# Raw keys and values for block maxima and sums: loads set 12 steps ahead of their batch, each sum in the step after its load

## The chip, the core and the metric

The kernel runs on one core of a Trainium2 chip. The core has TensorE (PE) for matrix products, VectorE (DVE), ScalarE (ACT) and GpSimd (POOL) for elementwise work, and SyncE (SP), which here only issues DMA transfers. Each engine works through its own list of instructions in order and waits for others by semaphores. The metric is the device time of one execution in microseconds. A change of less than 0.2% cannot be told from none here.

## The reference

Attention over a window and block summaries, followed by a feed-forward layer with a rational activation:

```python
# q, k, v: batch 4, heads 8, sequence 768, head size 64; block 32, window 16
k_sum = k.reshape(B, H, nb, block, D).max(axis=3)       # 24 block maxima of the keys
v_sum = v.reshape(B, H, nb, block, D).mean(axis=3)      # 24 block means of the values
scores_l = scale * q @ k^T, kept where |i - j| < 16
scores_s = scale * q @ k_sum^T + log(32)
a = softmax over both sets of scores
attn = a @ concat(v, v_sum)                             # 3072 tokens x 512
h = x @ w_in                                            # 512 -> 2048
P = a0 + a1*h + a2*h^2 + a3*h^3
Q = 1 + |b0|*|h| + |b1|*h^2
out = (P / (Q + 1e-6)) @ w_out                          # 2048 -> 512
```

## The kernel before

**Tiles.** The 3072 tokens are six groups of 512. The hidden width of 2048 is 16 slices (fc) of 128. A *step* is one slice of one group: `moe1` makes h (128x512) by twelve products, `gelu` turns it into a high and a low part gh and gl, and three steps later (`LAG`) `moe2` adds their products with the second weight matrix to the four output tiles po. So there are 96 steps and three more, numbered from 0; step 16 g + fc is tile `h{g}_{fc}`. A gelu is six passes of VectorE (L312, L315 to L319), five of ScalarE (L309 to L311, L313, L314) and one of GpSimd (L320, gl). The buffers of h, ta, tq and tu are double.

**Attention.** It runs in 48 half-blocks (jj) of 64 queries, 12 to a batch. The first eight are done ahead of step 0 (the ramp); the others are spread over the steps by `start_of(jj)`: two steps apart from half-block 16 on. In its step, a half-block's scores (sc) are multiplied, VectorE adds the mask and takes minima (L180), ScalarE exponentiates (L184), VectorE takes the reciprocal of the sums (L186, L187), GpSimd scales (L189, ss). In the next step TensorE transposes ss (L207, pt), once ahead of each output tile of `moe2`; the step after, the values are averaged (av).

**Block maxima and sums.** Batch 0 uses keys resident since the ramp. For batch 1, 2 and 3, `key_sum` loads four raw key tiles kr (128x768, 384 KB) and reduces each to 24 maxima (L118). For batches 2 and 3, `value_sum` loads four tiles vr (96x1024, 384 KB) and adds blocks of 32 (L126); batch 1 has its averages from TensorE. Keys of a batch are wanted when its first half-block is scored, at `start_of(12 bi)`: steps 7, 30 and 54; the values two steps later.

**Staging.** kr, vr, the halves of the weight slices 8 to 15 (wr, 512 KB each) and the outputs o of groups 0 to 4 share one pool `stage` of two buffers of 4 KB per partition, taken in turn. A half of a weight slice is rescaled by ScalarE (L281), shifted and joined by VectorE (L284, L285), copied by ScalarE (L288) and its remainder taken by GpSimd (L290).

**Order.** A scheduler places the instructions of each engine by priority and by its own estimate of when data is there. TensorE's list is pinned: `mm` and the transposes are held in the order in which they are written (`tc.keep_in_program_order`, which puts an instruction behind the one last written for its engine). VectorE's list is left to the scheduler. `todo` holds what is done beside the products of a step, entered by `at(step, function, ...)` and executed by `run` in three slots; `PRIO` shifts the priority of a function, and the sums are 15 places lower than they are written:

```python
KOFF = 6
VOFF = 5
PRIO = {"key_sum": -15, "value_sum": -15, "half_a": 40, "att_c": 40}
```

So the four key sums of batch 2 are written in steps 24 to 27 and the value sums in 25 to 28, those of batch 3 in 48 to 51 and 49 to 52, and those of batch 1 in 1 to 4; where they stand is the scheduler's choice.

Of the kernel before, what the change touches and what calls it, by code (L numbers as in the profile page):

```python
# [8 lines left out]
F32 = mybir.dt.float32  # L9
# [9 lines left out]
NB = S // BLK  # L19
# [23 lines left out]
NEARLY = 3  # L43
KOFF = 6
VOFF = 5
VLAG = 5
# [6 lines left out]
SLOT = {"att_c": 0, "half_a": 0, "att_b": 1}  # L53
PRIO = {"key_sum": -15, "value_sum": -15, "half_a": 40, "att_c": 40}
NHALF = NT // HQ
# [3 lines left out]
def tile_kernel(ctx, tc, qw_in, kraw, kwin, vpad, vred, wio, a, b, cmask, cident, cavg, out):  # L59
# [48 lines left out]

    def key_sum(bi, pr):
        if pr == 0:  # L110
            ksum[bi] = sp.tile([P, NPAIR, NB], F32, tag="ks", name=f"ks{bi}", bufs=2)
        if bi == 0:
            nc.sync.dma_start(out=kres[:, pr, :], in_=kraw[bi, pr])
            kr = kres[:, pr, WIN:WIN + S]
        else:
            kr = stage.tile([P, S], F32, tag="st", name=f"kr{bi}_{pr}")
            nc.sync.dma_start(out=kr, in_=kraw[bi, pr, :, WIN:WIN + S])
        nc.vector.tensor_reduce(ksum[bi][:, pr, :], kr.rearrange("p (n k) -> p n k", k=BLK), axis=AX.X, op=ALU.max)  # L118

    def value_sum(bi, c):  # L120
        if c == 0:
            vsum[bi] = sp.tile([NB * 4, NVC, VD], F32, tag="vs", name=f"vs{bi}", bufs=2)
        vs = vsum[bi]
        vr = stage.tile([NB * 4, VD, BLK], F32, tag="st", name=f"vr{bi}_{c}")
        nc.sync.dma_start(out=vr, in_=vred[bi, c])
        nc.vector.tensor_reduce(vs[:, c, :], vr, axis=AX.X, op=ALU.add)  # L126
        if c == NVC - 1:
            nc.vector.tensor_scalar_mul(vs, vs, 1.0 / BLK)
# [222 lines left out]
    for what in FIRST.split():  # L351
        n = int(what[1:] or 0)
        if what[0] == "Q":
            first_q(*((0, 2), (2, HPG))[n])
        elif what[0] == "K":
            key_sum(0, n)
        elif what[0] == "S":
# [37 lines left out]
    def run(step, slot):  # L395
        for f, args in todo.get((step, slot), ()):
            with tc.high_priority(offset=PRIO.get(f.__name__, 0)):
                f(*args)
# [12 lines left out]
    for jj in range(HPG, NHALF):  # L411
        at(start_of(jj) + 2, att_c, jj)
        at(start_of(jj), half_a, jj)
        at(start_of(jj) + 1, att_b, jj)
    for bi in range(1, B):
        for k in range(NPAIR):
            at(max(start_of(bi * NJ) - KOFF + k, 0), key_sum, bi, k)
        for k in range(NVC if bi > 1 else 0):
            at(max(start_of(bi * NJ) - VOFF + k, 0), value_sum, bi, k)
    for fc in range(NEARLY, NFC):  # L420
# [79 lines left out]
```

## Time and profile before

| What | Value |
|---|---|
| Median of 3 runs | 741.35 us (740.69 to 742.2) |
| The profiled execution's own time, its span | 740.98 us, 739.2 us |
| TensorE busy | 685.4 us (93%) |
| VectorE, ScalarE, GpSimd busy | 603.1, 471.1, 314.1 us |
| Mean granted TensorE clock | 0.962 |
| HBM read, written | 53.44 MB, 6.34 MB |

The profile is of one execution. Its page gives busy times, slices of the span, DMA queues, the chain of work that ended last, and the costliest groups of instructions; the trace behind it answers for single lines, tiles and stretches. A row of a timeline reads: start in us, duration, engine, line, operation, output and input tiles, count, and in brackets the engine's idle time before it with what ended it. A row of waits reads: who waited for whom, us in total, times, longest. A row of stretches reads: from:to, length, then busy us and instruction count of PE, PEld, DVE, ACT and POOL, the granted clock (1.00 is full), the DMA engines' busy share and GB/s; a stretch table for one line has that line's engine alone. A row of groups has count, busy us, mean ns of one, and the idle time just before them. A row of DMA issues has count, KB each and the median us from issue to landing.

### The profile page before, as it was taken

The numbers are of one execution on the slowest core, as the hardware profiler recorded it, in microseconds if no ns is written. First come the engines' busy times: TensorE is split into PE (matmuls) and PEld (weight loads), VectorE is DVE, ScalarE is ACT, GpSimd is POOL, SyncE is SP. The second block draws the span as 40 slices with busy tenths as digits, with TensorE's granted clock in tenths as the row PEclk, the third lists the DMA queues.
The fourth block names the chain that finished last, engine by engine and source line by source line (L and its number), as shares of the span: only waits on it lengthen the run. The fifth ranks groups of instructions, "written<-read, shape, count | busy, mean of one in ns | idle before, by whom it ended". The sixth has DMA issues, their size and how long they took to land.

```text
span 739.2 us, 12001 instructions
## 1 busy us (share of the span) xinstructions
PE 685.4 (93%) x4196; PEld 529.8 (72%) x4196; DVE 603.1 (82%) x1189; ACT 471.1 (64%) x1058; POOL 314.1 (42%) x328
## 2 busy tenths in 40 slices
PE   7875698899998999997999996999999999999997
PEld 4544476677776777775777775777777777888886
DVE  4588988997988878977778986877987887988885
ACT  2885667776765665774666774566776666675563
POOL 0676556653532444542343442534445343222231
PEclk9986599999999999999999999999999999999999
DMA  9984353512136101133110125111122110010001
GB/s 290 371 276 145 117 168 104 163 40 57 30 120 185 40 30 45 46 97 83 42 46 30 57 72 150 35 49 38 30 72 72 32 37 1 1 58 1 1 1 58
DMA packets 30681, 60.76 MB, mean 82 GB/s; under 512 B 3748, under 2 KB 15396, under 8 KB 29596
## 3 DMA queue, kind: packets, MB, share of 16 engines
q1 hardware_dynamic: 29916, 59.54, 25.5%
q8 instruction: 33, 0.54, 0.3%
q10 hardware_dynamic: 576, 0.25, 0.1%
q14 instruction: 28, 0.23, 0.1%
q0 software_dynamic: 128, 0.20, 0.1%
HBM read 53.44 MB, written 6.34 MB: 81 GB/s over the span
## 4 chain that ended last, share of the span: by engine, by line
PE 65%; DMA 14%; DVE 7%; POOL 5%; ACT 4%; issue 3%; SPq 0%; POOLq 0%; DVEq 0%; ACTq 0%
PE po L77 30%; PE h L77 28%; DMA wr<-in_wio_dram 5%; PE sc L77 4%; DMA kr<-in_kraw_dram 3%; PE av L77 2%; PE pt L207 2%; POOL ss L189 2%; DMA vr<-in_vred_dram 2%; DMA vr<-in_vpad_dram 1%; POOL w L290 1%; POOL wearly L290 1%; DVE tq L312 1%; DMA out_dram<-o 1%; ACT ss L184 1%
## 5 line engine op out<-in xcount | busy, mean ns | idle before, releaser
L320 POOL TENSOR_TENSOR gl<-tu,ta 128x512 fp32r<-128x512 f32 x96 | 133.7, 1393 | 232.3 <-DVE tu L319 145.6
L189 POOL TENSOR_SCALAR ss<-ss,sm 128x120 f32<-128x120 f32 x192 | 132.3, 705 | 143.2 <-ACT ta L314 93.6
L312 DVE SCALAR_TENSOR_TENSOR tq<-tq,cs,ta 128x512 f32<-128x512 f32 x96 | 109.9, 1145 | 51.8 <-ACT ta L310 51.2
L309 ACT ACTIVATE tq<-h 128x512 f32<-128x512 f32 x96 | 57.2, 596 | 133.0 <-PE h L77 131.4
L77 PE MATMUL po<-wearly,gh 128*128 128x512 f32 x384 | 134.3, 432 | 0.0
L77 PE MATMUL po<-w,gh 128*128 128x512 f32 x384 | 127.6, 413 | 0.0
L313 ACT ACTIVATE ta<-tq,cs 128x512 f32<-128x512 f32 x96 | 69.7, 726 | 73.2 <-DVE tq L312 72.3
L77 PE MATMUL h<-xh,wearly 128*128 128x512 f32 x384 | 102.4, 411 | 3.6 <-DVE tu L316 3.2
L77 PE MATMUL h<-xh,w 128*128 128x512 f32 x384 | 95.5, 391 | 0.0
L317 DVE SCALAR_TENSOR_TENSOR gh<-tu,cs,ta 128x512 fp32r<-128x512 f32 x96 | 73.7, 768 | 22.3 <-ACT ta L314 11.9
L77 PEld LDWEIGHTS h<-xh,wearly 128*128 128x128 f32 x384 | 75.2, 197 | 21.6 <-DVE tu L316 3.4
L207 PE MATMUL pt<-ident,ss 128*120 128x128 f32 x192 | 54.8, 296 | 33.2 <-POOL ss L189 31.8
L77 PEld LDWEIGHTS h<-xh,w 128*128 128x128 f32 x384 | 72.1, 188 | 16.1
L77 PEld LDWEIGHTS po<-wearly,gh 128*128 128x128 f32 x384 | 67.5, 198 | 18.0 <-issue 4.9
L319 DVE SCALAR_TENSOR_TENSOR tu<-tu,cs,tq 128x512 f32<-128x512 f32 x96 | 77.3, 806 | 3.0
L184 ACT ACTIVATE ss<-ss,sm 128x120 f32<-128x120 f32 x192 | 73.0, 383 | 10.0 <-DVE sm L180 10.0
L77 PE MATMUL po<-wearly,gl 128*128 128x512 f32 x192 | 78.0, 406 | 0.0
L77 PEld LDWEIGHTS po<-w,gh 128*128 128x128 f32 x384 | 65.7, 190 | 16.9 <-issue 2.7
L77 PE MATMUL po<-w,gl 128*128 128x512 f32 x192 | 75.5, 393 | 0.0
L311 ACT ACTIVATE tu<-h,cs 128x512 f32<-128x512 f32 x96 | 75.0, 781 | 0.0
L316 DVE SCALAR_TENSOR_TENSOR tu<-tu,cs,h 128x512 f32<-128x512 f32 x96 | 71.6, 746 | 2.8
L318 DVE SCALAR_TENSOR_TENSOR tq<-tq,gh 128x512 f32<-128x512 f32 x96 | 68.7, 716 | 2.9
(63 smaller groups left out, 1046.8 us busy)
## 6 DMA issues: line engine op xcount, KB each, us to landing
vw<-in_vpad_dram SPq DMA_DIRECT2D x44, 192.0 KB, 2.8
wr<-in_wio_dram SPq DMA_DIRECT2D x8, 1024.0 KB, 10.4
wr<-in_wio_dram SPq DMA_DIRECT2D x16, 512.0 KB, 4.0
kw<-in_kwin_dram SPq DMA_DIRECT2D x40, 192.0 KB, 2.6
out_dram<-o SPq DMA_DIRECT2D x24, 256.0 KB, 2.1
qw<-in_qw_dram SPq DMA_DIRECT2D x40, 128.0 KB, 2.7
kr<-in_kraw_dram SPq DMA_DIRECT2D x12, 384.0 KB, 3.5
vr<-in_vred_dram SPq DMA_DIRECT2D x8, 384.0 KB, 3.4
```

Of the source, the lines that this page charges most:

```text
L77: ins = nc.tensor.matmul(*args, **kw)
L184: nc.scalar.activation(ss[:, pr, :], ss[:, pr, :], AF.Exp, scale=-1.0, bias=sm[:, 0, pr:pr + 1], accum_out=sm[:, 1, pr:pr + 1])
L189: nc.gpsimd.tensor_scalar(ss[:, pr, :], ss[:, pr, :], sm[:, 1, pr:pr + 1], 1.0, op0=ALU.mult, op1=ALU.mult)
L207: ins = nc.tensor.transpose(out=pt[:NK, pr * P:(pr + 1) * P], in_=ss[:, pr, :], identity=ident)
L311: nc.scalar.activation(tu, h, AF.Identity, scale=cs[:, 3:4], bias=cs[:, 2:3])
L312: nc.vector.scalar_tensor_tensor(out=tq, in0=tq, scalar=cs[:, 5:6], in1=ta, op0=ALU.mult, op1=ALU.add)
L313: nc.scalar.activation(ta, tq, AF.Ln, bias=cs[:, 7:8])
L316: nc.vector.scalar_tensor_tensor(out=tu, in0=tu, scalar=cs[:, 1:2], in1=h, op0=ALU.add, op1=ALU.mult)
L317: nc.vector.scalar_tensor_tensor(out=gh, in0=tu, scalar=cs[:, 0:1], in1=ta, op0=ALU.add, op1=ALU.mult)
L318: nc.vector.scalar_tensor_tensor(out=tq, in0=tq, scalar=C1 * SH, in1=gh, op0=ALU.add, op1=ALU.mult)
L319: nc.vector.scalar_tensor_tensor(out=tu, in0=tu, scalar=cs[:, 0:1], in1=tq, op0=ALU.add, op1=ALU.subtract)
L320: nc.gpsimd.tensor_tensor(gl, tu, ta, op=ALU.mult)
```

## The change

`key_sum` and `value_sum` are each split into a load and a sum. The loads of batch bi are written from `s = start_of(12 bi) - 12` on, one per step: four of keys, then four of values (steps 18 to 25 for batch 2, 42 to 49 for batch 3; 0 to 3 for batch 1, which has keys alone). Each sum is written in the step after its load. It has no lowered priority any more and is pinned on VectorE behind the instruction written before it. In a step, `run` takes loads last.

```diff
-KOFF = 6
-VOFF = 5
+SOFF = 12
...
-PRIO = {"key_sum": -15, "value_sum": -15, "half_a": 40, "att_c": 40}
+LATE = ("key_load", "value_load")
+PRIO = {"half_a": 40, "att_c": 40}
...
+    sums = {}
+
-    def key_sum(bi, pr):
+    def key_load(bi, pr):
         if pr == 0:
             ksum[bi] = sp.tile([P, NPAIR, NB], F32, tag="ks", name=f"ks{bi}", bufs=2)
         if bi == 0:
...
         else:
             kr = stage.tile([P, S], F32, tag="st", name=f"kr{bi}_{pr}")
             nc.sync.dma_start(out=kr, in_=kraw[bi, pr, :, WIN:WIN + S])
-        nc.vector.tensor_reduce(ksum[bi][:, pr, :], kr.rearrange("p (n k) -> p n k", k=BLK), axis=AX.X, op=ALU.max)
-
-    def value_sum(bi, c):
+        sums["k", bi, pr] = kr
+
+    def key_sum(bi, pr):
+        kr = sums.pop(("k", bi, pr))
+        ins = nc.vector.tensor_reduce(ksum[bi][:, pr, :], kr.rearrange("p (n k) -> p n k", k=BLK), axis=AX.X, op=ALU.max)
+        if bi:
+            tc.keep_in_program_order(ins)
+
+    def value_load(bi, c):
         if c == 0:
             vsum[bi] = sp.tile([NB * 4, NVC, VD], F32, tag="vs", name=f"vs{bi}", bufs=2)
-        vs = vsum[bi]
         vr = stage.tile([NB * 4, VD, BLK], F32, tag="st", name=f"vr{bi}_{c}")
         nc.sync.dma_start(out=vr, in_=vred[bi, c])
-        nc.vector.tensor_reduce(vs[:, c, :], vr, axis=AX.X, op=ALU.add)
+        sums["v", bi, c] = vr
+
+    def value_sum(bi, c):
+        vs, vr = vsum[bi], sums.pop(("v", bi, c))
+        tc.keep_in_program_order(nc.vector.tensor_reduce(vs[:, c, :], vr, axis=AX.X, op=ALU.add))
         if c == NVC - 1:
             nc.vector.tensor_scalar_mul(vs, vs, 1.0 / BLK)
...
+            key_load(0, n)
             key_sum(0, n)
...
-        for f, args in todo.get((step, slot), ()):
+        for f, args in sorted(todo.get((step, slot), ()), key=lambda z: z[0].__name__ in LATE):
...
     for bi in range(1, B):
+        s = max(start_of(bi * NJ) - SOFF, 0)
         for k in range(NPAIR):
-            at(max(start_of(bi * NJ) - KOFF + k, 0), key_sum, bi, k)
+            at(s + k, key_load, bi, k)
+            at(s + k + 1, key_sum, bi, k)
         for k in range(NVC if bi > 1 else 0):
-            at(max(start_of(bi * NJ) - VOFF + k, 0), value_sum, bi, k)
+            at(s + NPAIR + k, value_load, bi, k)
+            at(s + NPAIR + k + 1, value_sum, bi, k)
```

The change shifts the line numbers: L118, L126, L180, L187, L312, L315 and L319 become L124, L137, L191, L198, L323, L326 and L330.

VectorE's list around steps 35 and 36 (tiles tq2_3 and tq2_4), before the change, in the middle of which the first two key sums of batch 3 stand:

```order
L312 SCALAR_TENSOR_TENSOR tq2_3_3183<-tq2_3_3183,cs_95,ta2_3_3182 128x512
L315 TENSOR_TENSOR tu2_3_3184<-tu2_3_3184,h2_3_3169 128x512
L316 SCALAR_TENSOR_TENSOR tu2_3_3184<-tu2_3_3184,cs_95,h2_3_3169 128x512
L118 TENSOR_REDUCE ks3_4087<-kr3_0_4088 128x24
L317 SCALAR_TENSOR_TENSOR gh2_3_3185<-tu2_3_3184,cs_95,ta2_3_3182 128x512
L318 SCALAR_TENSOR_TENSOR tq2_3_3183<-tq2_3_3183,gh2_3_3185 128x512
L319 SCALAR_TENSOR_TENSOR tu2_3_3184<-tu2_3_3184,cs_95,tq2_3_3183 128x512
L118 TENSOR_REDUCE ks3_4087<-kr3_1_4140 128x24
L312 SCALAR_TENSOR_TENSOR tq2_4_3236<-tq2_4_3236,cs_95,ta2_4_3235 128x512
```

With the change the same two sums stand at steps 43 and 44. The first is ahead of the gelu of step 44 (tq2_12):

```order
L328 SCALAR_TENSOR_TENSOR gh2_11_3708<-tu2_11_3707,cs_95,ta2_11_3705 128x512
L329 SCALAR_TENSOR_TENSOR tq2_11_3706<-tq2_11_3706,gh2_11_3708 128x512
L330 SCALAR_TENSOR_TENSOR tu2_11_3707<-tu2_11_3707,cs_95,tq2_11_3706 128x512
L124 TENSOR_REDUCE ks3_3689<-kr3_0_3690 128x24
L323 SCALAR_TENSOR_TENSOR tq2_12_3758<-tq2_12_3758,cs_95,ta2_12_3757 128x512
```

The second is behind the reciprocal of that step's half-block (sm31):

```order
L327 SCALAR_TENSOR_TENSOR tu2_12_3759<-tu2_12_3759,cs_95,h2_12_3744 128x512
L197 TENSOR_SCALAR sm31_3794<-sm31_3794 128x4
L198 RECIPROCAL sm31_3794<-sm31_3794 128x4
L124 TENSOR_REDUCE ks3_3689<-kr3_1_3742 128x24
L328 SCALAR_TENSOR_TENSOR gh2_12_3760<-tu2_12_3759,cs_95,ta2_12_3757 128x512
```

The sums of batches 2 and 3 alternate between these two places; they are written one in each of steps 19 to 26 and 43 to 50.

SyncE's list behind the ramp, before: the second and third raw key tiles of batch 1 are followed by the weight slices 7 and 8.

```order
L117 DMA kr1_1_823<-in_kraw_dram 128x768
L117 DMA kr1_2_900<-in_kraw_dram 128x768
L268 DMA wr7_0_826<-in_wio_dram 128x2048
L150 DMA vnext_107<-vn_595 24x512
L195 DMA vw0_100<-in_vpad_dram 96x512
L268 DMA wr8_0_904<-in_wio_dram 128x1024
L268 DMA wr8_1_906<-in_wio_dram 128x1024
L195 DMA vw1_101<-in_vpad_dram 96x512
L117 DMA kr1_3_998<-in_kraw_dram 128x768
```

And with the change:

```order
L119 DMA kr1_1_757<-in_kraw_dram 128x768
L279 DMA wr7_0_826<-in_wio_dram 128x2048
L161 DMA vnext_107<-vn_595 24x512
L206 DMA vw0_100<-in_vpad_dram 96x512
L206 DMA vw1_101<-in_vpad_dram 96x512
L168 DMA qw0_98<-in_qw_dram 128x256
L169 DMA kw0_96<-in_kwin_dram 128x384
L168 DMA qw1_99<-in_qw_dram 128x256
L169 DMA kw1_97<-in_kwin_dram 128x384
L119 DMA kr1_2_836<-in_kraw_dram 128x768
L279 DMA wr8_0_904<-in_wio_dram 128x1024
L206 DMA vw0_100<-in_vpad_dram 96x512
```

The third raw key tile and the first half of slice 8 have moved behind the window loads of half-blocks 10 and 11. The third tile's load waits for batch 1's first sum, which now stands ahead of the gelu of step 2.

## The prediction

> **What bounds the kernel now.** The page's first part says that TensorE is the bound: every other engine has idle time, and TensorE has next to none.
>
> ```profile
> PE 685.4 (93%) x4196; PEld 529.8 (72%) x4196; DVE 603.1 (82%) x1189; ACT 471.1 (64%) x1058; POOL 314.1 (42%) x328
> ```
>
> A share over the span hides where the missing 7% sits, so the next view is who waited for whom.
>
> ```profile
> PE pt L207 <- POOL ss L189: 31.8, 21, 5.7
> DVE ks L118 <- DMA kr<-in_kraw_dram: 10.2, 6, 4.0
> DVE vs L126 <- DMA vr<-in_vred_dram: 2.5, 4, 1.3
> ```
>
> TensorE's largest wait, 31.8 us, is for the transposes of the softmax weights. VectorE waits 10.2 and 2.5 us for the raw keys and values. The third view, busy time by stretch, shows that these belong together. The first three rows hold all sums of batches 2 and 3, the last two hold none; I cut them where a gelu's L315 starts, one per step, and the view of that line alone gives the steps as its counts.
>
> ```profile
> 210.17:261.57 51.40, 47.36 (x284) 36.76 (x284) 42.42 (x86) 31.38 (x77) 20.17 (x24) 1.00 0.39 119
> 317.05:362.67 45.62, 41.22 (x250) 31.77 (x249) 32.93 (x71) 27.21 (x64) 16.31 (x18) 0.96 0.29 85
> 430.59:478.12 47.53, 41.87 (x249) 31.93 (x248) 36.78 (x75) 27.23 (x64) 17.34 (x19) 0.93 0.33 99
> 362.67:430.59 67.92, 67.65 (x426) 53.15 (x425) 57.29 (x115) 44.51 (x104) 28.98 (x30) 1.00 0.13 40
> 478.12:545.14 67.02, 66.75 (x422) 52.53 (x421) 55.21 (x116) 44.42 (x104) 29.76 (x32) 1.00 0.14 40
> ...
> 210.17:261.56 51.39, 4.75 (x7) 1.00 0.39 120
> 317.05:362.66 45.61, 4.08 (x6) 0.96 0.29 85
> 430.59:478.11 47.52, 4.07 (x6) 0.93 0.33 100
> 478.12:545.13 67.01, 6.78 (x10) 1.00 0.14 40
> ```
>
> The clean stretches have ten steps each (the earlier one by the same count): 67.92 and 67.02, a mean of 6.75 us per step, with TensorE busy for all but 0.27 us. At that pace seven steps take 47.2 and six take 40.5. So the stretches with sums lose 51.40 - 47.2 = 4.2 (A), 45.62 - 40.5 = 5.1 (B) and 47.53 - 40.5 = 7.0 us (C), together **16.3 us**. TensorE idles 4.0, 4.4 and 5.7 of it; the rest goes with a granted clock of 0.96 and 0.93.
>
> The timeline of C shows the mechanism in order of time.
>
> ```profile
> 448.57 0.95 DVE L118 TENSOR_REDUCE ks<-kr 128x24 f32<-128x768 f32 x1 [4.00 <-DMA kr<-in_kraw_dram]
> ...
> 454.11 0.74 DVE L312 SCALAR_TENSOR_TENSOR tq<-tq,cs,ta 128x512 f32<-128x512 f32 x1
> ...
> 459.91 3.04 POOL L189 TENSOR_SCALAR ss<-ss,sm 128x120 f32<-128x120 f32 x3 [6.75 <-DVE sm L187]
> 460.33 0.47 PE L207 MATMUL pt<-ident,ss 128*120 128x128 f32 x1 [5.66 <-POOL ss L189]
> ```
>
> VectorE works in order. A sum whose data has not landed stops it for 4.00 us, a value sum behind it for 1.3 more (the longest of the 2.5 above); the gelu, the score minima and the reciprocal behind them come late, GpSimd scales late, and TensorE, whose transposes stand at fixed places between the products, stops for 5.66 us.
>
> **What the change removes.** No instruction goes: 12 key sums and 8 value sums stay, at these prices.
>
> ```profile
> L118 DVE TENSOR_REDUCE ks<-kr 128x24 f32<-128x768 f32 x12 | 11.4, 949 | 10.2 <-DMA kr<-in_kraw_dram 10.2
> L126 DVE TENSOR_REDUCE vs<-vr 96x32 f32<-96x1024 f32 x8 | 9.7, 1212 | 2.6 <-DMA vr<-in_vred_dram 2.5
> kr<-in_kraw_dram SPq DMA_DIRECT2D x12, 384.0 KB, 3.5
> vr<-in_vred_dram SPq DMA_DIRECT2D x8, 384.0 KB, 3.4
> ...
> 216.07 0.34 SPq L117 DMA_DIRECT2D kr<-in_kraw_dram  x1
> 221.42 0.75 DVE L319 SCALAR_TENSOR_TENSOR tu<-tu,cs,tq 128x512 f32<-128x512 f32 x1
> ```
>
> What changes is place. In the new order each sum of batches 2 and 3 stands in a step of its own, and its load waits for the sum two before it, two steps or 13.5 us earlier. Against 3.5 us to landing, that leaves 10 us for SyncE's queue, where the loads move past the window loads vw, qw and kw; those are wanted two or more steps later. Tightest is the first load of batch 2, which still waits for the output of group 0 (issued at 216.07, landed by 219.6); its sum moves behind the L319 that starts at 221.42, or 1.1 earlier without the sum and its wait that stand ahead of it now: it ends near 221.1, 1.5 us after the landing. I therefore cost the data waits at nothing and take all 16.3 us back: 740.98 - 16.3 = 724.7.
>
> **What it adds: one sum per step.** The sums stand at two places, right behind a reciprocal and right ahead of a gelu's L312. A clean pair of steps:
>
> ```profile
> 500.25 0.18 DVE L187 RECIPROCAL sm<-sm 128x4 f32<-128x4 f32 x1
> 503.99 1.22 DVE L312 SCALAR_TENSOR_TENSOR tq<-tq,cs,ta 128x512 f32<-128x512 f32 x1 [1.16 <-ACT ta L310]
> 510.00 1.26 DVE L312 SCALAR_TENSOR_TENSOR tq<-tq,cs,ta 128x512 f32<-128x512 f32 x1 [0.73 <-ACT ta L310]
> ...
> 500.60 2.81 POOL L189 TENSOR_SCALAR ss<-ss,sm 128x120 f32<-128x120 f32 x4 [3.41 <-ACT ta L314]
> ...
> 502.58 0.27 PE L207 MATMUL pt<-ident,ss 128*120 128x128 f32 x1
> ```
>
> The cover is VectorE's idle time for ScalarE: 1.16 + 0.73 = 1.9 us per pair of steps. Two key sums want 2 x 0.95 = 1.9 and fit. Two value sums want 2.4, so each pair of them leaves VectorE 0.5 us later, 1.0 after both. The transposes allow it: GpSimd's first quarter (2.81 / 4 = 0.70) is done at 501.30, TensorE takes it at 502.58, a slack of 1.3 us. Without that slack the eight half-blocks concerned would each give up to 1 us. I take 0.8 us in all, nearer to nothing, since batch 3's value sums meet the four extra passes of a group's split at step 48; the ends are 0 and 8.
>
> The SBUF — State Buffer page of the Trainium skill (section "SBUF: two separate sides") speaks against moving passes: VectorE instructions with two SBUF inputs and GpSimd's exclude each other for a whole instruction. The trace agrees for L312 (0.74 in C above, 1.22 beside GpSimd's product here).
>
> **What it adds at the end of C.** Values of batch 3 will hold both staging buffers when group 2 is written out at step 50; the output's second copy waits for the last value sum, which stands behind that step's reciprocal.
>
> ```profile
> 439.73 0.18 DVE L187 RECIPROCAL sm<-sm 128x4 f32<-128x4 f32 x1
> 439.91 1.15 ACT L340 COPY o<-po 128x512 f32<-128x512 f32 x2
> 442.88 0.59 ACT L340 COPY o<-po 128x512 f32<-128x512 f32 x1
> 443.53 0.73 PE L77 MATMUL po<-wearly,gh 128*128 128x512 f32 x2
> ```
>
> The second copy moves from 439.91 to the sum's end, 439.91 + 1.2 = 441.1. The fourth copy waits for the second's output, ends 1.2 us later than 443.47, and TensorE takes its bank at 443.53, so **+1.2 us** (0 to 2.5). Behind the waiting copy on ScalarE stand the third copy and the next gelu's squares, which have a step to spare.
>
> **What it moves at the start.** Batch 1's sums leave the ramp (three) and step 0 (one) for steps 1 to 4. Their raw keys keep both staging buffers until then: on SyncE the third load waits for the first sum, and behind it queue the halves of weight slices 8 to 15, which share the buffers. Each half carries its load, a rescaling and a copy on ScalarE, a shift and an or on VectorE and a difference on GpSimd, all four to five steps later: slice 8 at steps 3 and 4 instead of ahead of step 0, the last half of slice 15 at step 13 instead of 8.
>
> ```profile
> 59.06 0.94 DVE L118 TENSOR_REDUCE ks<-kr 128x24 f32<-128x768 f32 x1
> wr<-in_wio_dram SPq DMA_DIRECT2D x16, 512.0 KB, 4.0
> 65.56 1.23 PE L77 MATMUL h<-xl,wearly 128*128 128x512 f32 x4
> 69.94 0.59 ACT L309 ACTIVATE tq<-h 128x512 f32<-128x512 f32 x1
> 97.61 0.68 DVE L315 TENSOR_TENSOR tu<-tu,h 128x512 f32<-128x512 f32 x1
> 176.96 0.68 DVE L315 TENSOR_TENSOR tu<-tu,h 128x512 f32<-128x512 f32 x1
> 72.20:150.70 78.50, 62.45 (x362) 46.84 (x363) 71.21 (x146) 56.61 (x130) 47.04 (x46) 0.85 0.44 137
> 72.20:150.70 78.50, 8.98 (x14) 0.85 0.44 137
> ```
>
> Gain: two sums less ahead of the first product (2 x 0.94 = 1.9 us), and the first gelu no longer waits behind slice 8 from 66.79, the product's end, to 69.94 (3.1): 5.0 us. Loss: steps 0 to 9 took 78.50 us, 17.8 over nine steps of 6.75, with 14 half-slices split in them (the second row of the stretch counts their shifts), 1.27 us each with all that they carry; two more make 2.5, and three sums, in a stretch where VectorE is busy 71.21 of 78.50, are worth 0 to 2.9. So the start gains 2.5 us at most by this count and loses 0.4 at worst. By the pace of the halves instead: 14 in 78.5 is 5.6 us each. Step 3 comes at 97.6 - 5.0 - 3.5 halves of 1.27 = 88.2, sixteen halves of 5.6 from there end at 178, and gelu 13, behind which the last one stands, is at 177 now: no gain. At 5.0 us a half, nearer to the 4.0 of a landing, they end 8.8 us earlier. I take **-2 us**, between the counts; -9 to +6 for the range.
>
> **The sum.** 740.98 - 16.3 + 0.8 + 1.2 - 2.0 = 724.7 in terms of the profiled execution; the median of the runs is 0.37 above it: **725 us**.
>
> **The rivals.** (1) *VectorE becomes the bound where the sums now stand* (20%). For it: 1.9 us of idle time against 1.9 and 2.4 of work; and a pass that the sums push into GpSimd's work lasts 0.48 longer (1.22 against 0.74), 7.7 us over sixteen steps. Eight half-blocks late by up to 1 us come to the same: about 8 us given back, 733. Against it: the slack of 1.3 us. The exclusion that the Trainium skill states on its SBUF — State Buffer page is this rival's mechanism.
> (2) *The weights come late: slower* (8%). Place: products of slices 8 to 15 in steps 8 to 15. For it: the halves now begin at step 3, with two buffers, and gelu 13 needs a pace of 5.6 us. From 6.5 us per half (88.2 + 16 x 6.5 = 192, 15 past 177) it eats the whole gain; at 7 they end at 200, 23 past, and the time is 725 + 2 + 23 = 750. Against it: a load lands in 4.0 us, and slice 15 is due only at step 15.
> (3) *The change does not do what it says* (4%): the first loads of batches 2 and 3 stay behind the same outputs, so if it is the landing and not the sum's place that is late, the waits stay and the time is 741. Against it: in B the sums move eight steps behind their loads.
> (4) *The start gains more* (6%): fewer half-slices ahead of the first score blocks spare the stops there, -9 us in place of -2: 718.
>
> **How the numbers follow.** My forecast has 62%. The range must reach into (1) and (4): **717 to 735**. Faster by over 0.2% (1.5 us, about what a measurement of this kernel tells from none) are forecast, (1) and (4): 0.88; the same 0.04; slower 0.08.
>
> **What would show it.** Right: no wait of the sums for DMA in batches 2 and 3, TensorE's waits for scaled weights in A and B near zero, both stretches at 6.75 us per step, C with one wait of about 1 us for an output copy, the first gelu near 66. Wrong: transposes waiting around 1 us in every second step of 18 to 26 and 42 to 50; or products of slices 8 to 15 waiting for GpSimd's differences, with the step pace before step 15 above 9 us.

## The result

The changed kernel takes **724.14 us** (median of 4 runs, 723.83 to 725.74) against 741.67 us for the kernel before on the same chip (median of 4, 740.69 to 742.2). The ratio is 0.977, with a 95% interval of 0.975 to 0.979. In a second set of 5 runs it took 725.92 us (723.5 to 726.75), ratio 0.979 (0.976 to 0.981). The prediction of 725 us, with a range of 717 to 735, holds; several of its terms do not.

The profiled execution of the changed kernel took 723.93 us, with a span of 722.1 us. Engines first:

```profile
PE 682.8 (95%) x4196; PEld 527.2 (73%) x4196; DVE 602.3 (83%) x1189; ACT 472.0 (65%) x1058; POOL 313.7 (43%) x328
```

TensorE does the same work in a shorter span. The groups of the sums, whose last column is VectorE's idle time just before them:

```profile
L124 DVE TENSOR_REDUCE ks<-kr 128x24 f32<-128x768 f32 x12 | 11.2, 936 | 0.2 <-DMA kr<-in_kraw_dram 0.2
L137 DVE TENSOR_REDUCE vs<-vr 96x32 f32<-96x1024 f32 x8 | 9.6, 1196 | 0.0
```

Three rows of who waited for whom:

```profile
PE pt L218 <- POOL ss L200: 24.2, 18, 9.4
DVE tq L323 <- ACT ta L321: 43.6, 55, 3.8
ACT o L351 <- DVE vs L137: 0.4, 1, 0.4
```

The data waits went from 10.2 and 2.5 us to 0.2 and none. VectorE's idle time ahead of L323, from which the prediction took the room for the sums, shrank from 51.2 to 43.6 us. TensorE's wait for scaled weights fell from 31.8 to 24.2 us only, with a longest of 9.4 us where 5.7 was the longest before; 18.3 of the 24.2 lie between the first gelu and step 14, where it was 12.6. So stops went away in one place and appeared in another. The stretches say where; the first three are A, B and C, cut at the same gelus, the last three the start (steps 0 to 6, 6 to 9, 9 to 14):

```profile
211.47:257.72 46.25, 46.25 (x282) 36.25 (x281) 41.63 (x83) 31.16 (x77) 19.43 (x23) 1.00 0.44 132
312.84:352.54 39.70, 39.70 (x252) 30.93 (x250) 31.33 (x67) 27.24 (x64) 16.48 (x18) 1.00 0.28 87
419.87:461.13 41.26, 40.97 (x255) 31.60 (x256) 34.64 (x73) 27.14 (x64) 19.68 (x22) 1.00 0.22 72
66.10:107.51 41.41, 34.36 (x228) 25.72 (x227) 40.09 (x92) 31.52 (x76) 19.45 (x22) 0.93 0.40 118
107.51:136.59 29.08, 27.45 (x164) 20.89 (x163) 21.43 (x48) 19.25 (x44) 16.70 (x19) 0.93 0.42 129
136.59:184.11 47.52, 35.78 (x216) 27.15 (x215) 39.63 (x73) 30.44 (x64) 26.79 (x23) 0.86 0.36 107
```

In A and B TensorE has no idle time left, and in all three the granted clock is 1.00. A went from 51.40 to 46.25, B from 45.62 to 39.70, C from 47.53 to 41.26: 17.3 us together. The start is another matter. The first gelu stands at 66.1, 6.1 us earlier than before; by step 6 the change is 17.2 us ahead (107.51 against 124.72), and at step 14 it is 0.3 us behind (184.11 against 183.82). Steps 9 to 14, which took 33.1 us before, take 47.5. Here is one of the places where the lead goes:

```profile
147.08 0.68 ACT L292 ACTIVATE wr<-wr 128x512 f32<-128x512 f32 x1 [2.83 <-DMA wr<-in_wio_dram]
150.29 1.19 ACT L299 CAST w<-wr 128x512 fp32r<-128x512 f32 x2
151.00 3.02 POOL L301 TENSOR_TENSOR w<-wr,w 128x512 fp32r<-128x512 f32 x2 [6.66 <-ACT w L299]
151.09 0.17 DVE L198 RECIPROCAL sm<-sm 128x4 f32<-128x4 f32 x1
154.01 2.24 POOL L200 TENSOR_SCALAR ss<-ss,sm 128x120 f32<-128x120 f32 x4
154.86 0.47 PE L218 MATMUL pt<-ident,ss 128*120 128x128 f32 x1 [9.36 <-POOL ss L200]
```

TensorE stops for 9.36 us, from 145.50 on, for the scaled weights of a half-block. ScalarE waits 2.83 us for a half of a weight slice, with the exponentials of that half-block behind it in its list, so the reciprocal is ready only at 151.26. GpSimd's list has the differences of two such halves ahead of the scaling, which starts at 154.01, 2.75 us later.

### The profile page after: what moved, and what is told of

Same layout as the page of the kernel before. It is cut to its first block, busy times and chain, and to the rows that moved or that the text cites. A ratio compares the mean times of both kernels' runs of the same rounds, so it can differ in the third digit from the quotient of the medians.

```text
span 722.1 us, 12003 instructions
## 1 busy us (share of the span) xinstructions
PE 682.8 (95%) x4196; PEld 527.2 (73%) x4196; DVE 602.3 (83%) x1189; ACT 472.0 (65%) x1058; POOL 313.7 (43%) x328
## 4 chain that ended last, share of the span: by engine, by line
PE 75%; DVE 8%; DMA 5%; POOL 4%; ACT 4%; issue 3%; SPq 0%; POOLq 0%; DVEq 0%; ACTq 0%
PE po L77 32%; PE h L77 31%; PE sc L77 5%; DMA wr<-in_wio_dram 4%; PE pt L218 3%; PE av L77 3%; POOL ss L200 3%; PE vf L150 2%; POOL w L301 1%; DVE tq L323 1%; DVE wr L296 1%; DVE gh L328 1%; DVE tu L330 1%; DMA kres<-in_kraw_dram 1%; DVE tq L329 1%
## 5 line engine op out<-in xcount | busy, mean ns | idle before, releaser
L323 DVE SCALAR_TENSOR_TENSOR tq<-tq,cs,ta 128x512 f32<-128x512 f32 x96 | 114.0, 1188 | 44.1 <-ACT ta L321 43.6
L77 PE MATMUL po<-wearly,gh 128*128 128x512 f32 x384 | 131.0, 423 | 0.0
L77 PE MATMUL po<-w,gh 128*128 128x512 f32 x384 | 130.2, 420 | 0.0
L77 PE MATMUL h<-xh,wearly 128*128 128x512 f32 x384 | 100.3, 404 | 1.1 <-ACT xh L248 1.1
L77 PEld LDWEIGHTS po<-w,gh 128*128 128x128 f32 x384 | 67.2, 194 | 16.7 <-issue 3.3
L77 PEld LDWEIGHTS po<-wearly,gh 128*128 128x128 f32 x384 | 65.9, 193 | 17.1 <-issue 3.6
L218 PE MATMUL pt<-ident,ss 128*120 128x128 f32 x192 | 54.8, 296 | 24.4 <-POOL ss L200 24.2
L330 DVE SCALAR_TENSOR_TENSOR tu<-tu,cs,tq 128x512 f32<-128x512 f32 x96 | 74.0, 771 | 3.1
L77 PE MATMUL po<-wearly,gl 128*128 128x512 f32 x192 | 76.5, 399 | 0.0
```

Source lines behind the costliest of these rows:

```text
L77: ins = nc.tensor.matmul(*args, **kw)
L218: ins = nc.tensor.transpose(out=pt[:NK, pr * P:(pr + 1) * P], in_=ss[:, pr, :], identity=ident)
L323: nc.vector.scalar_tensor_tensor(out=tq, in0=tq, scalar=cs[:, 5:6], in1=ta, op0=ALU.mult, op1=ALU.add)
L330: nc.vector.scalar_tensor_tensor(out=tu, in0=tu, scalar=cs[:, 0:1], in1=tq, op0=ALU.add, op1=ALU.subtract)
```

## The experiments

The theory after the first reading had three parts. **Place**: the gain is that of A, B and C, since a sum that stands a step behind the one that frees its buffer finds its data. **Cover**: the sums fit into VectorE's idle time. **Start**: the lead is given back because batch 1's raw keys hold the two staging buffers, so that the halves of weight slices 8 to 15 come late. The rivals are named in the expectations.

The table has a row for each profiled execution; times are us. The first gelu and gelu 14 are read at the gelu passes that also cut the stretches above. These passes are VectorE's, and they shift by up to 4.5 us against TensorE where VectorE's order differs (at step 36 the gelu starts 7.41 us behind the last product of its h before the change, 2.86 us with it). So the last two columns are read on TensorE, from the end of the last product of h of one step to that of the other. Steps 18 to 36 hold the sums of batch 2, steps 36 to 55 those of batch 3 in most kernels. Steps 55 to 95 took 247.5 to 247.8 us in all of them.

| Kernel | Median | Gelu 0 | Gelu 14 | 18 to 36 | 36 to 55 |
|---|---|---|---|---|---|
| before | 741.67 | 72.2 | 183.8 | 126.3 | 142.4 |
| change | 724.14 | 66.1 | 184.1 | 121.7 | 129.6 |
| change, second set | 725.92 | 68.0 | 186.7 | 121.7 | 129.6 |
| batches 2, 3 only | 723.58 | 72.5 | 184.2 | 121.7 | 129.6 |
| batch 1 only | 744.43 | 69.4 | 187.5 | 129.0 | 141.5 |
| not pinned | 737.85 | 65.4 | 185.6 | 130.0 | 136.0 |
| pinned, two to a step | 731.03 | 70.0 | 187.5 | 127.2 | 129.8 |
| 9 steps ahead | 723.59 | 66.2 | 184.0 | 121.4 | 129.4 |
| short sums | 723.74 | 68.9 | 189.0 | 121.7 | 127.4 |
| batch 3 16 ahead | 729.20 | 67.0 | 184.1 | 121.8 | 132.6 |
| own buffer | 720.12 | 68.3 | 180.3 | 121.8 | 129.6 |
| no shift and join | 713.64 | 69.3 | 173.5 | 121.8 | 130.7 |
| own buffer, 18 ahead | 716.96 | 68.1 | 179.7 | 121.7 | 127.9 |
| the same, second halves later | 718.11 | 70.0 | 179.7 | 121.7 | 127.9 |

### Batches 2 and 3 only, and batch 1 only

`key_both` and `value_both` do a load of the change and its sum one behind the other. Here and in the next kernel they have the priority of -15 and no pin; the lines for that are left out of the cuts.

```diff
     for bi in range(1, B):
+        if bi == 1:   # load and sum together, priority -15, unpinned
+            for k in range(NPAIR):
+                at(max(start_of(bi * NJ) - 6 + k, 0), key_both, bi, k)
+            continue
```

> Batches 2 and 3 as in the change; batch 1 as before it (its key sums loaded and summed together, three ahead of step 0 and one in step 0, unpinned). Theory (the gain is that of stretches A, B and C alone; the changed start runs 17.2 us ahead at step 6 and gives all but 0.15 us of it back in steps 9 to 14): 741.67 - 17.0 = 724.7, within 1.5 us of the change's 724.1; steps 0 to 14 as long as before (111.6 us from gelu to gelu), all stretches from step 18 on as in the change. Rival 'the start earns 2 us, as the prediction's sum has it': 726.1. Rival 'batch 2 gains because batch 1 has moved': the waits of A stay, 728 or more.

Measured: 723.58 us (722.29 to 723.82), ratio 0.976 (0.974 to 0.978). The whole gain is there without the change of batch 1. The opposite kernel:

```diff
+        if bi > 1:    # load and sum together, priority -15, unpinned
+            for k in range(NPAIR):
+                at(start_of(bi * NJ) - 6 + k, key_both, bi, k)
+            for k in range(NVC):
+                at(start_of(bi * NJ) - 5 + k, value_both, bi, k)
+            continue
```

> Batch 1 as in the change; batches 2 and 3 as before it. Theory (the start nets nothing): 741.5, within 1.5 us of the kernel before, first gelu near 66 as in the change, 13 us ahead at step 9, nothing ahead at step 14, and the data waits of the sums (10.2 and 2.5 us) back. Rival 'the start earns 2 us': 739.7. Rival 'the start earns 9 us and the sums of batch 2 give it back': 733.

Measured: 744.43 us (742.99 to 746.6), ratio 1.004 (1.002 to 1.006): slower than before by 2.8 us, which none of the three readings had. The table says more than a single pair of runs. Eight profiled executions have the new start; their gelu 14 stands at 184.0 to 189.0, with a mean of 186.1. The two with the old start have it at 183.8 and 184.2. So the new start does not net nothing: on the mean it loses some 2 us, though three of the eight, at 184.0 to 184.1, lose nothing. The first gelu comes 4.7 us earlier on the mean (67.6 against 72.4), and steps 0 to 14 take 6.8 us more (118.4 against 111.6). Not all of the 2.8 us is the start's: steps 18 to 55 take 270.5 us on TensorE against 268.7 before, with the loss in batch 2, whose first sum waits 2.29 us for its data where it waited 0.25 us. How the new start brings that about was not followed; the profiled execution, at 746.6 us, is also the slowest of the eight.

### Early loads without the pin

```diff
-PRIO = {"half_a": 40, "att_c": 40}
+PRIO = {"half_a": 40, "att_c": 40, "key_sum": -15, "value_sum": -15}
...
-        if bi:
+        if bi == 1:
             tc.keep_in_program_order(ins)
...
-        tc.keep_in_program_order(nc.vector.tensor_reduce(vs[:, c, :], vr, axis=AX.X, op=ALU.add))
+        nc.vector.tensor_reduce(vs[:, c, :], vr, axis=AX.X, op=ALU.add)
```

> Loads of batches 2 and 3 written as early as in the change, but their sums no longer pinned and 15 places lower in priority, as before the change: the scheduler now sets them in steps 19 to 21 and 43 to 45, two or three to a step, where before it set them in 35 to 37. Theory 'place': a load still waits for the sum two before it, so a sum in the same step as that one stands 3.5 us or more of landing ahead of its data; eight sums in three steps wait 10 to 20 us in each batch, and the time is 735 to 760. Rival 'distance': that the loads come 12 steps ahead of the batch is what counts, the place of the sums does not: 724 to 727.

The steps in that text are wrong for batch 3: the scheduler set its eight sums in steps 35 to 37, where before the change three of them stood, with five more in 51 and 52. Measured: 737.85 us, ratio 0.994 (0.992 to 0.997). The data waits are back; the view of waits:

```profile
DVE ks L124 <- DMA kr<-in_kraw_dram: 8.2, 6, 2.4
DVE vs L137 <- DMA vr<-in_vred_dram: 2.1, 4, 1.0
```

So the early load by itself is worth little: steps 18 to 36 are slower than before (130.0 against 126.3). What is gained is in 51 and 52, which hold no sums now: the stretch from gelu 49 to gelu 55 takes 39.41 us, 8.1 less than before. Early loads do not take the waits away; the place of the sums decides.

### Pinned at the old distance, two to a step; and one to a step, 9 steps ahead

```diff
+        if bi > 1:    # as the old positions; pinned as in the change
+            for k in range(NPAIR):
+                at(start_of(bi * NJ) - 6 + k, key_both, bi, k)
+            for k in range(NVC):
+                at(start_of(bi * NJ) - 5 + k, value_both, bi, k)
+            continue
```

> Batch 1 as in the change. Loads and sums of batches 2 and 3 written where they were before the change (24 to 28 and 48 to 52, load and sum in one step, two sums in most), but pinned as in the change. Theory 'place' (a sum that stands a step or more behind the one that frees its buffer waits for no data, whatever the distance to the batch): no data wait in batch 2, steps 18 to 33 within 2 us of the change's 101.4 (before: 106.9); batch 3 meets group 2's outputs at step 50 and gives some of its gain back there; 726 to 734. Rival 'distance' (it takes loads 12 steps ahead of the batch): the data waits are back in both, 738 to 744.

Measured: 731.03 us, ratio 0.987 (0.984 to 0.990). The time is in the range of the theory, but its number for batch 2 failed: steps 18 to 33 took 106.8 us, as before the change, not 101.4. On TensorE the loss is in one step: from the end of the h of step 29 to that of step 30 it takes 11.84 us, 6.37 in the change. VectorE's timeline around steps 26 to 28, then GpSimd's and TensorE's, shows why:

```profile
273.77 1.22 DVE L137 TENSOR_REDUCE vs<-vr 96x32 f32<-96x1024 f32 x1 [1.94 <-DMA vr<-in_vred_dram]
...
281.60 0.95 DVE L124 TENSOR_REDUCE ks<-kr 128x24 f32<-128x768 f32 x1
282.46 1.21 DVE L137 TENSOR_REDUCE vs<-vr 96x32 f32<-96x1024 f32 x1
283.58 0.74 DVE L323 SCALAR_TENSOR_TENSOR tq<-tq,cs,ta 128x512 f32<-128x512 f32 x1
...
287.18 4.56 POOL L200 TENSOR_SCALAR ss<-ss,sm 128x120 f32<-128x120 f32 x4 [4.04 <-ACT ta L325]
288.11 0.47 PE L218 MATMUL pt<-ident,ss 128*120 128x128 f32 x1 [2.94 <-POOL ss L200]
```

The one wait for data in batch 2 is the 1.94 us of the first row. Further on two sums, some 2.1 us, stand ahead of L323, which finds ScalarE long done; the scaling comes late, and the transposes wait 2.94 us. How much of the loss is the wait and how much the two sums was not separated. Two to a step do not always cost: batch 3 has two or three of them in steps 49, 51 and 52, with waits for data of 3.0 us in all, and takes 129.8 us, where the change takes 129.6. Either more distance or one sum to a step might mend batch 2. The next run keeps the distance short and gives each sum its step:

```diff
-        s = max(start_of(bi * NJ) - SOFF, 0)
+        s = max(start_of(bi * NJ) - (9 if bi > 1 else SOFF), 0)
```

> The change with the loads of batches 2 and 3 written 9 steps ahead of their batch instead of 12, still one load and one pinned sum per step: sums of batch 2 in steps 22 to 29, of batch 3 in 46 to 53. Theory 'one sum to a step' (what the run with two pinned sums to a step lacked is room on VectorE, not distance): from gelu 18 to gelu 33 as in the change, 101.4 us within 1 (before 106.9, two to a step 106.8); batch 3 crosses group 2's outputs at step 50 and loses 2 to 5 us there; 726 to 730. Rival 'distance 12': 18 to 33 takes 104 or more, data waits of the sums are back, 731 to 741.

Measured: 723.59 us, ratio 0.976 (0.973 to 0.979), with no wait of these sums for data and 121.4 us from 18 to 36 (by the gelu passes 18 to 33 took 98.9 us, but the steps behind it give that back). So 12 steps of distance bring no more than 9: eight sums, pinned, each in a step of its own, have the whole gain at both. Distances under 9 with one sum to a step were not run. The loss at step 50 that the text expects was not there: 36 to 55 takes 129.4 us, the change 129.6.

### What the sums still cost

```diff
-        ins = nc.vector.tensor_reduce(ksum[bi][:, pr, :], kr.rearrange("p (n k) -> p n k", k=BLK), axis=AX.X, op=ALU.max)
+        ins = nc.vector.tensor_reduce(ksum[bi][:, pr, :], kr.rearrange("p (n k) -> p n k", k=BLK)[:, :, 0:2 if bi > 1 else BLK], axis=AX.X, op=ALU.max)
...
-        tc.keep_in_program_order(nc.vector.tensor_reduce(vs[:, c, :], vr, axis=AX.X, op=ALU.add))
+        tc.keep_in_program_order(nc.vector.tensor_reduce(vs[:, c, :], vr[:, :, 0:2], axis=AX.X, op=ALU.add))
```

> The change, with each sum of batches 2 and 3 reading 2 of its 32 elements (so block maxima and sums of these batches are of two tokens); places, loads and waits stay. It takes some 15 us of VectorE's work away. Theory 'cover' (the pinned sums fit into VectorE's idle time; the prediction gives them 0.8 us, and 1.2 for the output copy that waits for one): 722 to 724. Rival 'VectorE is the bound where the sums stand': 8 us less, 714 to 717.

Measured: 723.74 us (721.77 to 726.77), with a start that came out slowest of the eight. From step 18 to step 55 TensorE takes 249.2 us, in the change 251.4: the sums of both batches cost **2.2 us**, none of it in batch 2. Nearly all of it lies in one step: from the end of the h of step 49 to that of step 50 the change takes 8.14 us, this kernel 6.04. There the change's VectorE works through group 3's split and two value sums without a pause of over 0.2 us, the score block comes late, and one of its four scalings lasts long. GpSimd's view of the tile ss (durations as least, median and longest, ns) and the timeline of the change:

```profile
L200 POOL TENSOR_SCALAR ss<-ss,sm x4: 360/528/2037, 417.1 to 420.1; 128x120 f32<-128x120 f32 x4
...
417.80 0.33 PE L218 MATMUL pt<-ident,ss 128*120 128x128 f32 x1 [1.15 <-POOL ss L200]
417.90 0.73 DVE L329 SCALAR_TENSOR_TENSOR tq<-tq,gh 128x512 f32<-128x512 f32 x1
418.55 0.74 DVE L323 SCALAR_TENSOR_TENSOR tq<-tq,cs,ta 128x512 f32<-128x512 f32 x1
419.21 0.74 DVE L330 SCALAR_TENSOR_TENSOR tu<-tu,cs,tq 128x512 f32<-128x512 f32 x1
419.87 0.68 DVE L326 TENSOR_TENSOR tu<-tu,h 128x512 f32<-128x512 f32 x1
420.16 0.33 PE L218 MATMUL pt<-ident,ss 128*120 128x128 f32 x1 [0.53 <-POOL ss L200]
```

TensorE stops twice, for 1.15 and 0.53 us. The second stop is for a scaling that lasted 2.04 us beside three VectorE passes in a row. The copy of the output that waits for a value sum, 0.4 us on ScalarE, stops no product.

### Batch 3 moved away from the output copies

```diff
-        s = max(start_of(bi * NJ) - SOFF, 0)
+        s = max(start_of(bi * NJ) - (16 if bi == 3 else SOFF), 0)
```

> The change with the loads of batch 3 written 16 steps ahead of it instead of 12: its sums stand in steps 39 to 46, none near step 50, where group 2's output copies use the two staging buffers. Theory 'collision' (in the change the output copies and values of batch 3 share the buffers at steps 48 to 52): from gelu 49 to gelu 55 it takes 41.26 us in the change and 39.4 in a run whose sums of batch 3 stood in steps 35 to 37, so 1.9 us less: 722.2, the prediction's term for it being 1.2 (722.9). Rival 'the sums cost the same wherever they stand': 724 within 0.7.

Measured: 729.20 us (727.01 to 730.71), ratio 0.985 (0.982 to 0.988): **slower** than the change, which neither reading had. On TensorE steps 48 to 55 are 2.2 us shorter (47.6 against 49.8), close to the 1.9 of the theory, but steps 44 to 48 take 31.7 us in place of 26.6. That is 2.9 us more in all in the profiled execution, which at 727.01 us was the fastest of the five. GpSimd's view of the tile ss there, for the change and for this kernel, and then this kernel's timeline:

```profile
L200 POOL TENSOR_SCALAR ss<-ss,sm x4: 364/578/877, 401.1 to 402.6; 128x120 f32<-128x120 f32 x4
```

```profile
L200 POOL TENSOR_SCALAR ss<-ss,sm x4: 363/881/4660, 401.9 to 408.3; 128x120 f32<-128x120 f32 x4
```

```profile
403.64 0.68 DVE L258 TENSOR_TENSOR xl<-x,xh 128x512 fp32r<-128x512 f32 x1
404.24 0.68 DVE L329 SCALAR_TENSOR_TENSOR tq<-tq,gh 128x512 f32<-128x512 f32 x1
404.84 1.88 DVE L258 TENSOR_TENSOR xl<-x,xh 128x512 fp32r<-128x512 f32 x3
406.65 0.74 DVE L330 SCALAR_TENSOR_TENSOR tu<-tu,cs,tq 128x512 f32<-128x512 f32 x1
407.31 0.74 DVE L323 SCALAR_TENSOR_TENSOR tq<-tq,cs,ta 128x512 f32<-128x512 f32 x1
407.98 0.67 DVE L326 TENSOR_TENSOR tu<-tu,h 128x512 f32<-128x512 f32 x1
...
408.34 0.47 PE L218 MATMUL pt<-ident,ss 128*120 128x128 f32 x1 [3.46 <-POOL ss L200]
```

One scaling of a quarter lasts 4.66 us, where in the change the four of the same half-block last 0.36 to 0.88 each. It ends at 408.3, after seven VectorE passes in a row that read two tiles in SBUF, 0.3 us after VectorE takes L326, one of whose inputs (h) is in PSUM. In the change the four quarters were done by 403.5 (402.6 + 0.9), ahead of the split's passes. Here they began 0.8 us later (401.90 against 401.09), with value sums where the change has key sums, and the third met the split. The 2.04 us in the change's step 49 has the same picture: three such passes in a row, and the end 0.2 us after L326 starts. The SBUF — State Buffer page of the Trainium skill (section "SBUF: two separate sides") says that a VectorE instruction with two SBUF inputs and a GpSimd instruction that reads SBUF exclude each other, the later one blocked fully; the trace agrees, and these two scalings lasted over a whole row of such instructions. It is not always so: a product of GpSimd (gl) that started at 404.91 in the change, within the split's passes, ended after 1.57 us, and one of the passes took 1.78 us in its place. The reading was not isolated in a run of its own.

### The start

First, batch 1's raw keys out of the staging buffers:

```diff
-            kr = stage.tile([P, S], F32, tag="st", name=f"kr{bi}_{pr}")
+            if bi == 1 and pr == 0:
+                sums["k1"] = wm.tile([P, NPAIR, S], F32, tag="wm", name="k1")
+            kr = sums["k1"][:, pr, :] if bi == 1 else stage.tile([P, S], F32, tag="st", name=f"kr{bi}_{pr}")
```

> The change, but the four raw key tiles of batch 1 go to a buffer of their own (a late-weight buffer of the wm pool that is free until slice 10), not to the two staging buffers. Sums of batch 1 in steps 1 and 4; three halves of slices 8 and 9 are split ahead of step 0, three more by step 1, the last at step 11 instead of 13. Theory 'buffers' (the start gives its lead back because the halves of slices 8 to 15 wait for raw keys in the staging buffers and then stand ahead of the score blocks in steps 9 to 13): the lead at step 14 is no longer 0, time 714 to 721. Rival 'work' (sixteen halves cost the same wherever they stand): 723 to 726, first gelu later by some 3 us and steps 9 to 14 shorter by as much.

Measured: 720.12 us (719.83 to 721.63), ratio 0.972 (0.970 to 0.974). Gelu 14 stands at 180.3, where the eight runs with shared buffers had 184.0 to 189.0; the buffers cost 4 to 9 us. The first gelu is within their spread. But at step 6 this kernel is 11.8 us ahead of the one before (112.96 against 124.72) and at step 14 3.5, so the buffers are not all. Second, VectorE's work on the halves left out:

```diff
-                for i in range(n):
+                for i in range(n if fc < NSTG else 0):
                     l32, h32 = raw[:, i, :, 0], raw[:, i, :, 1]
```

> The change without VectorE's two passes (shift and join) on the sixteen halves of weight slices 8 to 15: these keep only their upper words, so their values are wrong; loads, ScalarE's and GpSimd's work stay. 16 x (0.73 + 0.90) = 26 us of VectorE's work go from steps 3 to 13. Theory 'work' (what eats the lead of the start is VectorE's work on the halves, which moves but does not shrink): more than 8 us less, 704 to 716, with step 14 at 164 to 176. Rival 'landing' (the halves wait for buffers, loads and the copies behind them): 3 us less at most, 721 to 724.

Measured: 713.64 us, ratio 0.964 (0.961 to 0.966), gelu 14 at 173.5. The stretches from gelu 0 to gelu 14 of the kernel before, the change, the own buffer and this kernel, one fence each (VectorE's busy time is the third of the five):

```profile
72.21:183.82 111.61, 95.57 (x583) 73.06 (x584) 98.50 (x205) 78.60 (x180) 62.36 (x60) 0.89 0.35 109
```

```profile
66.10:184.11 118.01, 97.59 (x604) 73.75 (x603) 101.15 (x210) 81.22 (x184) 62.94 (x62) 0.90 0.39 116
```

```profile
68.34:180.29 111.95, 94.00 (x585) 71.50 (x586) 98.88 (x207) 79.29 (x180) 66.22 (x62) 0.93 0.33 99
```

```profile
69.29:173.52 104.23, 94.06 (x606) 71.92 (x605) 84.27 (x180) 80.59 (x184) 62.29 (x62) 0.95 0.42 132
```

VectorE has the same 98 to 101 us to do in these fourteen steps in the first three. Where the halves come early they slow steps 0 to 9 and leave 9 to 14 clean (before: 33.1 us), where they come late it is the other way round. With 17 us less of that work (the 26 of the text was too high) the stretch is 14 us shorter. So both parts are shown: the work on the halves moves and does not shrink, and the shared buffers add a loss of their own. Whether the 14 us are VectorE's time itself or the waits of the passes behind it in each half's chain was not separated.

### A faster kernel

The own buffer, with batch 3 at 18 steps ahead: its sums then stand in steps 37 to 44, clear of the split too.

```diff
-        s = max(start_of(bi * NJ) - SOFF, 0)
+        s = max(start_of(bi * NJ) - (18 if bi == 3 else SOFF), 0)
```

> The change with batch 1's raw keys in a buffer of their own, and the loads of batch 3 written 18 steps ahead, so that its sums stand in steps 37 to 44, clear of group 3's split at step 48 and of group 2's outputs at step 50. Theory 'collision': from gelu 44 to gelu 55 it takes some 73.8 us, as in the run whose sums of batch 3 stood in 35 to 37 (74.6 in the change; 78.3 with the sums in 39 to 46, where GpSimd's scaling met the split's passes): 719 from the 720.1 of the own buffer alone. Rival 'the sums shift what the split's passes meet': 722 to 725.

Measured: **716.96 us** (715.46 to 717.84), ratio 0.967 (0.964 to 0.969): 24 us faster than the kernel before, and some 7 to 9 faster than the change. Steps 36 to 55 take 127.9 us, 0.4 more than with sums cut short. Then the second half of each weight slice three steps later (`w_load` takes the half as an argument):

```diff
+            at(fc - CVL + 3, lambda fc: w_split(fc, w_load(fc, 1)), fc)
```

> As the run with the own buffer and batch 3 written 18 steps ahead, but of each weight slice 8 to 15 the second half (the one of the second matrix, wanted three steps later) is loaded and split three steps later. The halves then end at step 12 instead of 11 and stand one or two to a step. Theory 'work' (VectorE's work in steps 0 to 13 bounds the start; its place matters little): within 1.5 us of that run. Rival 'order' (halves ahead of their need block score blocks that are wanted): 2 to 5 us less.

Measured: 718.11 us (716.43 to 718.77), with gelu 14 at 179.7 in both. The place of the halves inside the start made no difference. The change itself, run beside these:

> The change itself once more, beside the three others. All theories: 724.1 within 1.5, with gelu 14 at 184 to 189 (five profiled runs with this start had it at 184.1, 184.1, 185.6, 187.5 and 189.0), and from gelu 18 on the times of the first run within 0.5 us per stretch.

Measured: 725.92 us, gelu 14 at 186.7; steps 18 to 55 agree with the first run within 0.1 us. Nearly all that differs between the two profiled executions of one program lies ahead of step 18.

## Why the prediction was right, point by point

**What bounds the kernel, and the mechanism: right.** TensorE's stops in A, B and C came from sums that waited for data at the head of VectorE's list. Of the signs named, four are there: no wait for data of the sums of batches 2 and 3, no stop of the transposes in A and B, a pace near 6.75 us per step in both (cut on TensorE, A takes 47.48 us for seven steps and B 40.26 for six, 6.78 and 6.71), and the first gelu at 66.1 (65.4 to 70.0 in all runs with this start). The fifth is not: C has no stop for an output copy, but stops for transposes in step 49.

**The 16.3 us: too small.** On TensorE the change is 17.3 us shorter from step 18 to step 55 (251.4 against 268.7), and 19.5 with the sums cut short (249.2). The pace did not fail; the cut did. A, B, C and the whole from step 18 to 55, cut at the ends of the last products of h, for the kernel before; then the whole for the change; then A, B and C for the kernel with short sums:

```profile
207.45:259.45 52.00, 47.96 (x310) 37.41 (x311) 44.13 (x93) 32.22 (x78) 19.65 (x22) 1.00 0.40 122
314.19:360.63 46.44, 42.04 (x254) 32.40 (x254) 34.31 (x70) 27.20 (x64) 17.14 (x21) 0.96 0.29 83
427.73:476.14 48.41, 42.75 (x254) 32.72 (x253) 37.08 (x74) 27.22 (x64) 17.75 (x21) 0.93 0.33 98
207.45:476.14 268.69, 253.60 (x1570) 196.69 (x1570) 217.43 (x443) 167.32 (x394) 107.51 (x115) 0.98 0.25 74
```

```profile
207.78:459.14 251.36, 248.96 (x1571) 194.15 (x1570) 218.56 (x443) 167.84 (x394) 107.96 (x115) 1.00 0.27 79
```

```profile
212.70:260.20 47.50, 47.50 (x310) 37.40 (x311) 38.53 (x90) 32.11 (x78) 19.75 (x22) 1.00 0.43 132
314.90:355.16 40.26, 40.26 (x254) 31.41 (x254) 32.40 (x67) 27.24 (x64) 17.05 (x20) 1.00 0.27 87
421.58:461.87 40.29, 40.29 (x254) 31.44 (x253) 33.95 (x71) 27.25 (x64) 17.52 (x21) 1.00 0.23 74
```

The last three rows, 128.05 us in all and without idle time on TensorE, are what nineteen clean steps take; at 6.75 the prediction had 128.2. With the change, the sums in full, A, B and C take 130.2. Before, the three stretches took 146.85 us on TensorE and 144.55 between the gelu passes: these lay 2.7 to 2.9 us behind TensorE's products where the stretches begin and 2.0 to 2.1 where they end, so 2.3 us of the loss fell outside the cuts. A further 0.7 us went in step 47, outside all three (6.72 us against 6.04 in the change), for a cause that was not looked for. Of the 17.3 us, 12.7 are idle time of TensorE (15.1 against 2.4) and 4.6 are the same products in less busy time, with a granted clock of 1.00 in place of 0.98.

**The tightest load: right.** SyncE issued the first load of batch 2 at 217.36, 1.3 us later than before; the sum behind L330 starts without a wait for data, though with 0.5 us of room and not the 1.5 of the prediction (217.36 + 3.5 = 220.9):

```profile
217.36 0.34 SPq L119 DMA_DIRECT2D kr<-in_kraw_dram  x1
...
220.67 0.75 DVE L330 SCALAR_TENSOR_TENSOR tu<-tu,cs,tq 128x512 f32<-128x512 f32 x1
221.34 0.94 DVE L124 TENSOR_REDUCE ks<-kr 128x24 f32<-128x768 f32 x1
```

**The 0.8 us for the sums and the 1.2 for the output copy: right in sum, 2.2 against 2.0, wrong in parts.** Key and value sums of batch 2 cost nothing (121.7 us from 18 to 36 with the full sums and with short ones), and no transposes stop there. The slack of 1.3 us, which the prediction gives them, was nearer 1.1: it took 0.70 us, a mean, for the first quarter, which lasted 0.87. Batch 3 pays some 2.1 in one step, where its value sums stand right behind the split (the place the prediction named, priced too low), and next to nothing for the output copy, whose wait of 0.4 us stops no product. That a full VectorE would take the gain back (the first rival) is wrong for one sum per step. With two to a step batch 2 lost its whole gain, in one step and behind a wait of 1.94 us for data, and batch 3 lost none.

**The -2.0 us for the start: wrong, the sign too.** Measured is a loss of some 2 us (gelu 14 at 186.1 on the mean against 184.0) and, between the medians of the kernels with and without it, 0.6 to 2.8, of which not all is the start's. The 5.0 us ahead of the first gelu came, 4.7 on the mean. The count of halves failed, "two more make 2.5": halves that are split later are not saved. And the pace of the halves was put at 5.0 to 5.6 us. ScalarE's rescaling of the first and the last:

```profile
83.36 0.68 ACT L292 ACTIVATE wr<-wr 128x512 f32<-128x512 f32 x1 [0.80 <-DMA wr<-in_wio_dram]
178.57 0.69 ACT L292 ACTIVATE wr<-wr 128x512 f32<-128x512 f32 x1 [0.16 <-POOL gl L331]
```

Fifteen intervals in 95.2 us are 6.3 us each, close to the 6.5 from which the second rival was to eat the gain. That rival had the mechanism, late halves, but the wrong victim: steps 9 to 14 ran at 9.5 us each, yet no product waited for its weights; score blocks queued behind the halves on ScalarE and GpSimd, and their transposes stopped TensorE. So the total of 725 came out close by luck: from step 18 on the forecast was -16.3 + 0.8 + 1.2 = -14.3 where -17.3 was measured, and at the start -2 where some +2 was, two errors of 3 and 4 us with opposite signs.

## What to carry to other kernels

When a pass at the head of a full engine's list waits for a transfer through a buffer taken in turn, give it a place of its own one step behind the pass that frees the buffer; here one sum per step had the whole gain at 9 and at 12 steps of distance, and early loads without such places had little. Before work is moved into a busier stretch, ask which other transfers take the same buffers and what is queued behind them on every engine: the lead at one marker is no gain until the work that was put off has been paid for. Cut stretches by marks on the engine that bounds the kernel: passes of another engine shift against it, and here they hid 2.3 us of the loss.

## What the runs showed of the hardware that was not expected

A GpSimd scaling of 120 columns, 0.36 to 0.88 us in the same half-block of the change, lasted 4.66 us beside seven VectorE passes in a row with two SBUF inputs; moving the sums of batch 3 by four steps was enough to bring the two together, and it cost 5.1 us in four steps. A shorter case, 2.04 us beside three such passes, stands in the change itself, in both of its profiled executions. And the start varies from run to run: in eight executions of seven kernels, with the same order of instructions up to there, gelu 14 stood anywhere from 184.0 to 189.0, while the 77 steps from gelu 18 to the last agree within 0.2 us in two executions of the change (498.44 and 498.30).
